# A four-row matmul operand padded to 128 rows, tap weights turned by matmul, and a new written-out order in a one-core SSM and MLP kernel

## The chip, the cores and the metric

The kernel runs on one core of one Trainium2 chip. A core has five engines that run their own instruction streams side by side: TensorE (PE: matmuls and the weight loads for them), VectorE (DVE), ScalarE (ACT), GpSimd (POOL) and SyncE (SP, which here only issues DMAs). They share a scratch memory of 128 rows (partitions), and TensorE writes its results to eight accumulator banks (PSUM). Engines wait for each other and for DMAs on semaphores. The metric is the device time of one execution in microseconds, median of several runs.

## The reference

Two branches over the same input x = A_q (2048 positions, 640 channels, bf16) are mixed by a sigmoid gate:

```python
def _A_ref(q, k, v, shift_k, ssm_k, ssm_D):
    k_pad = jnp.pad(k, ((0, 0), (ks - 1, 0), (0, 0)))
    for t in range(ks):                                   # ks = 4
        k_shift = k_shift + k_pad[:, t:t + S, :] * shift_k[:, ks - 1 - t][None, None, :]
    kv = k_shift * v
    y = irfft2(rfft2(pad(kv)) * rfft2(pad(ssm_k)))[..., :S, :]   # causal convolution per channel
    y = y + kv * ssm_D[None, None, :]
    return q * y

def _B_ref(x, w1, w2, w3, w4):
    h = _gelu(_layernorm(x, axis=-1) @ w1)                # 640 x 640
    # the four quarters of h are shifted by 1, -1, 2, -2 positions
    hs = jnp.concatenate([g0, g1, g2, g3], axis=-1) @ w2  # 640 x 640
    x1 = x + hs
    h2 = _gelu(_layernorm(x1, axis=-1) @ w3) @ w4         # 640 x 1536 x 640
    return x1 + h2

g = _sigmoid((x * gate_w).sum(-1, keepdims=True))
return g * a + (1 - g) * b
```

## The kernel before, in words

All 2048 positions are held in the core's memory as 16 row tiles of 128 (X). The work falls into groups that bear the name of the function that issues them.

Branch B. `x_load` (L843) brings X in; `ln1` (L853) normalises a tile with VectorE's statistics instructions and turns it to channels-first, the first eight tiles by TensorE transposes (L866), the others by SyncE transposing DMAs. `mm1` (L873) is the first product. It has five column blocks: blocks 0 to 3 are the first 128 columns of each quarter, and the fifth block (`w1x`) collects the last 32 columns of all four quarters, so that its gelu is four instructions of 32 rows with four different shifts. The loop at L1066 cuts mm1 into widths of 128 positions for the first chunk of 512 (the fifth block in 256), 256 for the second, 512 for the last two. `mmg` (L887) makes the gate's dot products; `mm2` (L905) the second product, whose result VectorE adds to X (L919) from tile 4 on; `ln2` (L923) normalises again and turns by DMA; `mm3` (L928) and `mm4` (L949) are the MLP; `base` (L944) writes scaled x1.

Branch A. `h_load`, `h_fold` and `h_chunk` (L745) make the spectrum of the filter, 128 channels at a time in five chunks: the 2048 taps are cut into four blocks of 512, folded into even and odd halves on VectorE, turned by DMA, and multiplied with constant DFT matrices on TensorE. `h_fold` also copies row 0 of the turned result to a small tile `hsp` (L743). `h_chunk` uses it as the moving operand of a correction of four rows, whose stationary operand `Zs` is four rows too:

```python
    Zs = AR[0:4, oUT + 4224:oUT + 4480].rearrange("p (j f) -> p j f", j=2)
    hsp = [AR[0:4, o:o + 512] for o in (oUT + 4480, oUT + 4992)]
...
                    if r == 0:
                        pairs.append((Zs[:, j, :], ex))
```

This comes to two matmuls of four rows by 512 columns in each of five chunks. The DFT constants around `Zs` are loaded by the DMA `Rh` from a table of 1920 columns over all rows, `Zs` among them. `kv_load` and `kv_chunk` (L777) do the same for k and v, with the four taps of the shift as per-channel scalars `wk`; `x_fwd` (L790) is their transform; `combine` and `unit` (L960 on) the products of the spectra on VectorE with accumulating DMAs from GpSimd; `final` (L1021) the inverse transform, 16 groups, which TensorE, ScalarE and VectorE finish and which SyncE or GpSimd write or accumulate to the output.

At the start, VectorE sets constants, among them a tile of ones of 640 columns (L671) in which `warm` matmuls run (WARM = 15, L675), and 26 `fill` matmuls (L679) are strewn among the first real ones; none of them makes a result that is used. The taps `shift_k` (640 x 4) are brought by a DMA to `wkb` in channel order (128 rows, five groups of four elements of two bytes, so runs of 8 bytes) and copied to `wk`. `dcol` (L710) turns `ssm_D` and `gate_w`, each loaded as five rows of 128, into columns by two matmuls with five rows.

What sets the order: the program is first recorded as a list of operations, each with the tiles that it reads and writes. The list SEQUENCE, written out by hand as numbers, then gives the order in which they are issued, over all engines and DMA queues; each engine runs its own share of that list in order. The list PLACES gives each accumulator tile its bank. `schedule` (L255) adds to the first user of a bank a wait for the last reader of the tile that held it, and `emit` (L276) turns all dependences into semaphore waits, leaving out those that are implied. Helpers record most instructions, so that matmuls have the line L647, VectorE's tensor-tensor operations L627, ScalarE's L637 and DMAs L238 or (transposes) L235.

Of the kernel before, what the change touches and what calls it, by code (L numbers as in the profile page):

```python
# [422 lines left out]
def bass_gated_mix__ssm_conv_h3__mixer_s_mlp__prompt_kernel(  # L423
# [23 lines left out]
    def V(o, n):  # L447
        return AR[:, o:o + n]
# [7 lines left out]
    def ps(n, cls):  # L456
# [3 lines left out]
    SEQUENCE = [74, 1, 11, 54, 76, 53, 9, 0, 12, 73, 5, 13, 75, 14, 67, 15, 156, 57, 80, 16, 157, 81, 17, 56, 61, 96,  # L460
# [59 lines left out]

# [645 lines left out]
```

## Time and profile before

| what | value |
|---|---|
| median of 3 runs | 229.17 us (228.46 to 234.25) |
| profiled execution | 229.3 us, its span 227.5 us |
| TensorE busy | 217.7 us, 96% of the span, 1437 matmuls |
| VectorE busy | 205.8 us, 90% |
| ScalarE busy | 175.5 us, 77% |
| GpSimd busy | 96.1 us, 42% |
| TensorE idle for VectorE's tensor-tensor operations | 1.4 us, three times |
| TensorE idle for w1's DMA | 0.7 us, once |

The times of the trace count from the start of the span in microseconds. A row of a group gives line, engine, operation, the tiles written and read, the shape, the count, then busy time and the mean length of one in ns, and the idle time of the engine just ahead of such instructions with what ended it. A row of the timeline gives start, length, engine, line and how many instructions follow each other there. Matmuls overlap: the time from issue to issue is shorter than the length of one. The chain that ended last goes from the last instruction back, at each step to what released it.

### The profile page before, as it was taken

How to read it: one execution, taken by the hardware profiler on the slowest of the kernel's cores; microseconds unless marked ns; L12 is line 12 of the kernel's file. 1: busy time of each engine (PE TensorE's matmuls, PEld its weight loads, DVE VectorE, ACT ScalarE, POOL GpSimd, SP SyncE). 2: the span in 40 equal slices, each digit the busy share in tenths (PEclk: the TensorE clock that was granted, in tenths of full speed). 3: DMA queues.
4: the chain of work that ended last, by engine and by line, in shares of the span. 5: the costliest groups of instructions: out<-in, count | busy, mean ns of one | idle time of the engine just before them, and what ended most of it. 6: DMA issues, size and time to landing. Idle time of an engine off the chain costs nothing.

```text
span 227.5 us, 3881 instructions
## 1 busy us (share of the span) xinstructions
PE 217.7 (96%) x1437; PEld 128.5 (56%) x1437; DVE 205.8 (90%) x339; ACT 175.5 (77%) x315; POOL 96.1 (42%) x111
## 2 busy tenths in 40 slices
PE   6989999999999999999999999999999999999970
PEld 2578776554445644446764466665477644677730
DVE  5989998989988989799999999989899999996691
ACT  2279899799999779999976995838987379745970
POOL 0332333263014340000147648297696344357771
PEclk9999999999999999999999999999999999999995
DMA  5999999999999998999679999799999999989997
GB/s 168 280 233 314 197 260 225 179 223 265 216 178 248 194 294 184 278 218 148 179 158 126 208 238 186 158 168 173 269 191 145 240 181 185 176 113 129 124 135 129
DMA packets 81007, 45.01 MB, mean 198 GB/s; under 512 B 59976, under 2 KB 75868, under 8 KB 80988
## 3 DMA queue, kind: packets, MB, share of 16 engines
q1 hardware_dynamic: 71560, 31.92, 62.4%
q0 software_dynamic: 9264, 12.78, 38.2%
q8 instruction: 11, 0.18, 0.3%
q10 hardware_dynamic: 164, 0.07, 0.1%
q14 instruction: 8, 0.07, 0.1%
HBM read 14.92 MB, written 6.55 MB: 94 GB/s over the span
## 4 chain that ended last, share of the span: by engine, by line
PE 88%; DVE 4%; DMA 3%; SPq 2%; ACT 1%; issue 1%
PE PSall L647 86%; DVE arena L627 4%; DMA arena<-in_B_w_dram 3%; SPq L238 2%; PE PSall L679 1%; ACT arena L637 1%; PE PSall L866 1%
## 5 line engine op out<-in xcount | busy, mean ns | idle before, releaser
L647 PE MATMUL PSall<-arena 128*128 128x320 bf16 (+5 forms) x1354 | 205.8, 310 | 2.1 <-DVE arena L627 1.4
L647 PEld LDWEIGHTS PSall<-arena 128*128 128x128 bf16 (+1 forms) x1354 | 122.1, 98 | 85.8 <-issue 6.4
L627 DVE TENSOR_TENSOR arena<-arena 128x2560 bf16<-128x2560 bf16 (+6 forms) x198 | 160.8, 863 | 8.9 <-ACT arena L637 7.0
L637 ACT ACTIVATE arena<-PSall 128x512 bf16<-128x512 f32 (+7 forms) x182 | 105.4, 626 | 26.1 <-PE PSall L647 18.2
L637 ACT ACTIVATE arena<-arena 128x640 bf16<-128x640 bf16 (+5 forms) x75 | 53.9, 740 | 9.2 <-DVE arena L627 8.2
L815 POOL TENSOR_TENSOR arena<-arena 128x1 f32<-128x1 f32 (+2 forms) x17 | 22.6, 1338 | 45.4 <-DVE arena L826 37.7
L238 POOL DMA_DIRECT2D out_dram<-arena x28 | 32.6, 1446 | 19.9 <-ACT arena L637 10.6
L637 ACT ACTIVATE arena<-PSall,arena 128x640 bf16<-128x640 f32 (+1 forms) x32 | 20.6, 655 | 10.2 <-PE PSall L647 10.0
L238 POOL DMA_DIRECT2D arena<-arena x15 | 19.1, 1332 | 18.8 <-DVE arena L627 14.8
L627 POOL TENSOR_TENSOR arena<-arena 128x4 bf16<-128x4 bf16 (+3 forms) x26 | 15.5, 606 | 22.2 <-DVE arena L627 19.4
L632 DVE TENSOR_SCALAR arena<-arena 128x640 bf16<-128x640 bf16 (+3 forms) x45 | 23.3, 541 | 0.9 <-POOL arena L815 0.6
L632 POOL TENSOR_SCALAR arena<-arena 128x2 f32<-128x2 f32 (+4 forms) x21 | 14.4, 689 | 19.9 <-DVE arena L627 9.5
L811 DVE BATCH_NORM_STATS2 arena<-arena 128x6 f32<-128x320 bf16 x32 | 14.3, 477 | 2.3 <-DMA arena<-in_A_q_dram 2.1
L919 DVE SCALAR_TENSOR_TENSOR arena<-PSall,arena 128x640 bf16<-128x640 f32 x12 | 9.7, 817 | 1.6 <-PE PSall L647 1.6
L675 PE MATMUL PSall<-arena 128*128 128x512 bf16 x15 | 5.8, 574 | 1.7 <-DVE arena L671 1.7
L679 PE MATMUL PSall<-arena 128*128 128x512 bf16 x26 | 7.4, 379 | 0.0
L675 PEld LDWEIGHTS PSall<-arena 128*128 128x128 bf16 x15 | 2.0, 139 | 5.1 <-issue 3.2
L866 PE MATMUL PSall<-arena 128*128 128x128 bf16 x40 | 3.4, 219 | 0.0
L866 PEld LDWEIGHTS PSall<-arena 128*128 128x128 bf16 x40 | 2.7, 98 | 0.5
L679 PEld LDWEIGHTS PSall<-arena 128*128 128x128 bf16 x26 | 2.3, 97 | 1.1
L637 ACT ACTIVATE PSall<-PSall 128x640 f32<-128x640 f32 x4 | 2.8, 708 | 0.0
L812 DVE BATCH_NORM_AGGREGATE arena<-arena 128x2 f32<-128x12 f32 x16 | 2.8, 194 | 0.0
(26 smaller groups left out, 10.5 us busy)
## 6 DMA issues: line engine op xcount, KB each, us to landing
arena<-arena POOLq DMA_DIRECT2D x12, 640.0 KB, 6.4
arena<-in_A_q_dram SPq DMA_DIRECT2D x14, 320.0 KB, 4.8
out_dram<-arena POOLq DMA_DIRECT2D x20, 160.0 KB, 4.5
arena<-in_A_ssm_k_dram SPq DMA_DIRECT2D x5, 512.0 KB, 4.5
arena<-in_B_w_dram SPq DMA_DIRECT2D x4, 480.0 KB, 4.6
out_dram<-arena SPq DMA_DIRECT2D x10, 160.0 KB, 4.2
arena<-in_B_w_dram SPq DMA_DIRECT2D x1, 1152.0 KB, 6.0
out_dram<-arena SPq DMA_DIRECT2D x12, 80.0 KB, 2.4
```

The lines of the kernel that those rows point to most:

```text
L238: fn = lambda e: e.dma_start(out, in_, **kw)
L627: P.op(eng, lambda e: e.tensor_tensor(o, real(a), real(b), op), [a, b], [o], dve_ns(o, [a, b], 2) if eng == "dve" else 500)
L632: P.op(eng, lambda e: e.tensor_scalar(o, real(a), s1, s2, op0=op0, **({} if op1 is None else {"op1": op1})), [a] + aps, [o], dve_ns(o, [a] ...
L637: P.op("act", lambda e: e.activation(real(o), real(a), f, bias=bias, scale=scale, **({"accum_out": accum} if accum is not None else {})), ...
L647: fns.append(lambda e, l=l, r=r, i=i: e.matmul(real(o), l, r, start=(i == 0), stop=(i == last)))
L675: P.op("pe", lambda e: e.matmul(real(pw), warm[:, 0:128], warm[:, 128:640], start=True, stop=True), [warm], [pw], 427.0 if i < 14 else 216.0)
L679: P.op("pe", lambda e: e.matmul(real(pw), warm[:, 0:128], warm[:, 128:640], start=True, stop=True), [warm], [pw], 216.0)
L811: P.op("dve", lambda e, o=o, i=i: e.bn_stats(o, i), [i], [o], 400)
L812: P.op("dve", lambda e: e.bn_aggr(bna[:, t, :], bns[k]), [bns[k]], [bna[:, t, :]], 120)
L815: P.op("pool", lambda g: g.tensor_tensor(o, a, e, ALU.pow), [a, e], [o], dur)
L866: P.op("pe", [lambda e, c=c, pb=pb, xn=xn: e.transpose(real(pb)[:, 128 * c:128 * (c + 1)], xn[:, 128 * c:128 * (c + 1)], ident) for c in r ...
L919: P.op("dve", lambda e: e.scalar_tensor_tensor(x, real(pr), 1.0, x, op0=ALU.mult, op1=ALU.add, accum_out=st[1, 0][:, t:t + 1]), [pr, x], [ ...
```

## The change

- The four-row operands `Zs` and `hsp` become tiles of 128 rows. `hsp` is zeroed once at the start by VectorE; the DMA of `h_fold` still writes its rows 0 to 3. The rows of `Zs` below the fourth come with the table that holds it.
- `shift_k` is loaded as five rows of 512 elements (128 channels with four taps each) beside `ssm_D` and `gate_w`. Four five-row matmuls with a stride of four turn the taps to columns in an accumulator tile, from which `wk` is copied. `wkb` goes.
- The tile of ones has 512 columns, not 640.
- The fifth column block of mm1 is done once for each chunk of 512 positions.
- 20 fillers, not 26.
- SEQUENCE and PLACES are written anew. In the new order the X rows and shift_k stand ahead of w1 in SyncE's queue and two more rows of X between w1's halves; 5 of 20 fillers, before 15 of 26, stand behind the first matmul that needs w1's second half; mm2 of tile 12 is followed directly by a part of h_chunk 3 in the same banks (PLACES 0); nine finals, before eight, have their inverse transform behind the last mm4.

```diff
-    SEQUENCE = [74, 1, 11, 54, 76, 53, 9, 0, 12, 73, 5, 13, 75, 14, 67, 15, 156, 57, 80, 16, 157, 81, 17, 56, 61, 96,
...
+    SEQUENCE = [71, 1, 13, 52, 70, 5, 6, 12, 14, 53, 73, 7, 9, 0, 2, 11, 15, 50, 72, 8, 16, 49, 149, 17, 148, 77, 18,
...
-    Zs = AR[0:4, oUT + 4224:oUT + 4480].rearrange("p (j f) -> p j f", j=2)
-    hsp = [AR[0:4, o:o + 512] for o in (oUT + 4480, oUT + 4992)]
+    Zs = V(oUT + 4224, 256).rearrange("p (j f) -> p j f", j=2)
+    hsp = [V(o, 512) for o in (oUT + 4480, oUT + 4992)]
...
-    dg5 = AR[0:5, oXN + 640:oXN + 896]
+    dg5 = AR[0:5, oXN + 512:oXN + 1280]
...
-    wkb = bfs[:, 0:20].rearrange("p (c j) -> p c j", c=5)
...
+    for h in hsp:
+        P.op("dve", lambda e, h=h: e.memset(h, 0.0), [], [h], 230)
     WARM = 15
-    FILL = 26
+    FILL = 20
     const("warm")
-    P.op("dve", lambda e: e.memset(V(oXN, 640), 1.0), [], [V(oXN, 640)], 230)
-    warm = V(oXN, 640)
+    P.op("dve", lambda e: e.memset(V(oXN, 512), 1.0), [], [V(oXN, 512)], 230)
+    warm = V(oXN, 512)
...
     const("shk")
-    P.dma(sp, wkb, A_shift_k.rearrange("(c p) j -> p c j", p=128), slow=True)
+    P.dma(sp, dg5[:, 256:768], A_shift_k.rearrange("(c p) j -> c (p j)", p=128))
...
     const("taps")
-    ts(wk, wkb, 1.0, None, ALU.mult)
+    pk = ps(1, "set")[:, 0:20].rearrange("p (j c) -> p j c", j=4)
+    P.op("pe", [lambda e, j=j: e.matmul(real(pk)[:, j], dg5[:, 256 + j:768:4], ident[0:5, 0:5], start=True, stop=True) for j in range(4)],
+         [dg5[:, 256:768], ident], [pk], 120)
+    ts(wk, pk.rearrange("p j c -> p c j"), 1.0, None, ALU.mult)
...
-        P.dma(sp, hsp[c % 2].rearrange("p (a n) -> p a n", a=1), het[c % 2][0:1].rearrange("p e b c -> p e (b c)"))
+        P.dma(sp, hsp[c % 2][0:4].rearrange("p (a n) -> p a n", a=1), het[c % 2][0:1].rearrange("p e b c -> p e (b c)"))
...
             for t in range(4):
                 at(mm1, 0, 128 * t, 128, range(4))
-                if t % 2:
-                    at(mm1, 0, 128 * (t - 1), 256, (4,))
+            at(mm1, 0, 0, 512, (4,))
         else:
             n = 256 if sc < 2 else 512
             for t in range(512 * sc, 512 * sc + 512, n):
-                at(mm1, sc, t, n)
+                at(mm1, sc, t, n, range(4))
+            at(mm1, sc, 512 * sc, 512, (4,))
```

More of the change, by code (lines that the diff above doesn't have):

```diff
@@ L458, in ps @@
         return v if n == 1 else v.rearrange("p (b n) -> p b n", b=2)
-    SEQUENCE = [74, 1, 11, 54, 76, 53, 9, 0, 12, 73, 5, 13, 75, 14, 67, 15, 156, 57, 80, 16, 157, 81, 17, 56, 61, 96,
[59 rows of a table removed]
-    PLACES = [0, 1, 6, 3, 2, 1, 7, 4, 7, 3, 3, 5, 6, 5, 4, 5, 6, 7, 1, 1, 1, 1, 1, 2, 2, 5, 6, 6, 3, 5, 4, 4, 0, 7, 2,
[5 rows of a table removed]
+    SEQUENCE = [71, 1, 13, 52, 70, 5, 6, 12, 14, 53, 73, 7, 9, 0, 2, 11, 15, 50, 72, 8, 16, 49, 149, 17, 148, 77, 18,
[58 rows of a table added]
+    PLACES = [0, 5, 1, 4, 2, 3, 4, 5, 2, 6, 1, 7, 6, 5, 7, 5, 6, 4, 6, 7, 2, 1, 0, 3, 5, 1, 3, 7, 5, 3, 7, 2, 4, 4, 4,
[5 rows of a table added]
     HW = S + 4
@@ L667, in bass_gated_mix__ssm_conv_h3__mixer_s_mlp__prompt_kernel @@
         P.op("dve", lambda e, i=i: e.memset(krev[i][:, :, :, 0:1], 0.0), [], [krev[i][:, :, :, 0:1]], 70)
+    for h in hsp:
+        P.op("dve", lambda e, h=h: e.memset(h, 0.0), [], [h], 230)
     WARM = 15
-    FILL = 26
+    FILL = 20
     const("warm")
-    P.op("dve", lambda e: e.memset(V(oXN, 640), 1.0), [], [V(oXN, 640)], 230)
-    warm = V(oXN, 640)
+    P.op("dve", lambda e: e.memset(V(oXN, 512), 1.0), [], [V(oXN, 512)], 230)
+    warm = V(oXN, 512)
     pw = ps(1, "warm")
     for i in range(WARM):
-        P.op("pe", lambda e: e.matmul(real(pw), warm[:, 0:128], warm[:, 128:640], start=True, stop=True),
+        P.op("pe", lambda e: e.matmul(real(pw), warm[:, 0:128], warm[:, 0:512], start=True, stop=True),
              [warm], [pw], 427.0 if i < 14 else 216.0)
@@ L678, in bass_gated_mix__ssm_conv_h3__mixer_s_mlp__prompt_kernel @@
         const("fill%d" % i)
-        P.op("pe", lambda e: e.matmul(real(pw), warm[:, 0:128], warm[:, 128:640], start=True, stop=True), [warm], [pw], 216.0)
+        P.op("pe", lambda e: e.matmul(real(pw), warm[:, 0:128], warm[:, 0:512], start=True, stop=True), [warm], [pw], 216.0)
     const("gelu")
@@ L710, in bass_gated_mix__ssm_conv_h3__mixer_s_mlp__prompt_kernel @@
     P.op("pe", [lambda e, i=i: e.matmul(real(pr)[:, 5 * i:5 * i + 5], dg5[:, 128 * i:128 * (i + 1)], ident[0:5, 0:5], start=True, stop=True) for i in range(2)],
-         [dg5, ident], [pr], 60)
+         [dg5[:, 0:256], ident], [pr], 60)
     act(dgT, pr, ACTF.Copy)
```

127 rows, old and new, of tables (PLACES, SEQUENCE) are left out of this document.

## The prediction

> **What bounds the kernel now.** I read the head of the page first, then the chain that ended last in order of time, then the waits of TensorE.
>
> ```profile
> span 227.5 us, 3881 instructions
> PE 217.7 (96%) x1437; PEld 128.5 (56%) x1437; DVE 205.8 (90%) x339; ACT 175.5 (77%) x315; POOL 96.1 (42%) x111
> GB/s 168 280 233 314 197 260 225 179 223 265 216 178 248 194 294 184 278 218 148 179 158 126 208 238 186 158 168 173 269 191 145 240 181 185 176 113 129 124 135 129
> PEclk9999999999999999999999999999999999999995
> ```
>
> TensorE is busy for 96% of the span at an undisturbed clock. VectorE at 90% is the nearest other bound; ScalarE and the queues are farther off. The chain, in order of time, says where the busy engine is also the one that sets the end:
>
> ```profile
> 4.58 7.51 DMA arena<-in_B_w_dram
> 12.09 0.14 issue
> 12.23 0.44 PE PSall L647 x5
> ...
> 29.23 182.58 PE PSall L647 x1133
> ...
> 222.73 0.49 DVE arena L627
> ```
>
> From 12.23, when the second half of w1 has landed, the chain is TensorE alone to 211.8 us, one piece of it 182.58 us and 1133 matmuls long with no other engine between. Behind that a tail of ScalarE, VectorE and the last write ends the span. So an instruction's worth of TensorE time that is saved anywhere from 12 to 212 us comes off the end whole, unless the next operand is late then. The waits of TensorE:
>
> ```profile
> PE PSall L675 <- DVE arena L671: 1.7, 1, 1.7
> PE PSall L647 <- DVE arena L627: 1.4, 3, 0.9
> PE PSall L647 <- DMA arena<-in_B_w_dram: 0.7, 1, 0.7
> ```
>
> The 1.7 is the start (the ones for the warming matmuls), the 1.4 stands in the tail, and the 0.7 is the w1 wait at 12.23. That is all: the present order is without stalls, so any wait that the new order adds shows in full.
>
> **The change part by part.** All sums are made against the profiled execution, 229.3 us (span 227.5 and 1.8 outside it), which stands 0.1 from the median 229.17.
>
> *Padding the four-row operand.* First what a full matmul takes from issue to issue, then a stretch with one matmul of four rows in it:
>
> ```profile
> 87.73 2.54 PE L647 MATMUL PSall<-arena 128*128 128x512 bf16 x11
> 79.93 1.45 PE L647 MATMUL PSall<-arena 128*128 128x512 bf16 x5
> L647 PE MATMUL PSall<-arena 128*128 128x512 bf16 x4 | 1.2, 382 | 0.0
> L647 PE MATMUL PSall<-arena 4*128 4x512 bf16 x1 | 0.4, 385 | 0.0
> L647 PE MATMUL PSall<-arena 4*128 4x512 bf16 x10 | 3.8, 385 | 0.0
> ```
>
> Eleven in 2.54 us, the last 0.38 of it one matmul's own length: (2.54 - 0.38) / 10 = 0.216 each. The second stretch is five, and the two rows under it (the same window by shape) show that one of them has four rows: 1.45 - 0.385 - 4 x 0.216 = 0.20 us more than five full ones take. The durations are alike, 382 and 385 ns, so the loss lies between the instructions, on entering and on leaving the small shape. With all 128 rows nothing changes shape: 10 x 0.20 = **-2.0 us**, all ten standing before 90 us where TensorE is saturated. [...]
>
> Its price is two memsets of 128x512 on VectorE at the very start:
>
> ```profile
> 1.07 0.59 DVE L671 MEMSET arena<- 128x640 bf16 x1
> 3.43 2.86 DVE L811 BATCH_NORM_STATS2 arena<-arena 128x6 f32<-128x320 bf16 x6 [1.71 <-DMA arena<-in_A_q_dram]
> ```
>
> At most 2 x 0.59, at least half that; VectorE idles 1.71 us ahead of 3.43 for its first input, which hides either. I take 0; if they stood ahead of the ones instead, TensorE would start up to 1.2 us late. The ones themselves shrink from 640 to 512 columns, 0.12 of 0.59 us: **-0.1 us** at the start.
>
> *Taps turned by matmul.* Two five-row matmuls stand between fillers already:
>
> ```profile
> 7.62 0.59 PE L679 MATMUL PSall<-arena 128*128 128x512 bf16 x2
> 8.15 0.20 PE L710 MATMUL PSall<-arena 5*128 5x5 bf16 x2
> 8.28 0.60 PE L679 MATMUL PSall<-arena 128*128 128x512 bf16 x2
> ```
>
> From 7.62 to 8.28 is 0.66 us; two fillers take 0.43 of it, so the pair costs 0.23. A second one inside the pair adds about 0.04, so four cost **+0.3 us**, on the path because they now stand among the first product's matmuls, behind w1.
>
> *Fillers.* 26 become 20:
>
> ```profile
> 9.13 1.46 PE L679 MATMUL PSall<-arena 128*128 128x512 bf16 x6
> 10.84 0.72 PE L866 MATMUL PSall<-arena 128*128 128x128 bf16 x10
> ```
>
> (1.46 - 0.38) / 5 = 0.216 again. Six fewer are **-1.3 us**, if TensorE has work to put there. In the old order 15 fillers stand behind the w1 wait, in the new one 5, so ten go from the saturated part and four are added before the wait, which the next item counts.
>
> *The w1 wait.* The last ten matmuls before it issue from 10.84 on at 0.056 each (0.72 less the last one's own 0.22, over 9), so TensorE has nothing from 11.40 to 12.23: 0.83 us lost before. In the new order it has 5 more fillers and 5 more transposes and 5 fewer one-column matmuls (0.025 each) ahead of the first matmul on the second half: 11.40 + 1.08 + 0.28 - 0.12 - 0.12 (earlier start) = 12.5 us. SyncE's queue:
>
> ```profile
> 4.07 1.04 SPq L238 DMA_DIRECT2D arena<-in_B_w_dram  x2
> 5.15 0.92 SPq L238 DMA_DIRECT2D arena<-in_A_shift_k_dram  x1
> 6.11 2.95 SPq L238 DMA_DIRECT2D arena<-in_B_w_dram  x1
> ```
>
> The old order sends both halves at 4.07 and 4.58. The new one puts two more rows of X (320 KB) between them and takes one 40 KB piece of w2 away; 280 KB at the 280 GB/s of the second slice is 1.0 us, so the half lands at 12.09 + 1.0 = 13.1. The wait becomes 0.6: **-0.2 us** net. That shift_k no longer costs the queue its 0.92 and then most of the 2.95 helps what is queued behind it, nothing on the path by itself.
>
> *Fifth block in 512s.* The columns are the same, and so is TensorE's time. ScalarE's four-row gelus go from the first form to the second:
>
> ```profile
> L637 ACT ACTIVATE arena<-PSall 32x256 bf16<-32x256 f32 x16 | 5.9, 374 | 0.4 <-PE PSall L647 0.3
> L637 ACT ACTIVATE arena<-PSall 32x512 bf16<-32x512 f32 x8 | 4.7, 588 | 0.3 <-PE PSall L647 0.2
> ```
>
> 5.9 us in sixteen become 4.7 in eight, -1.2 on an engine 77% busy: hidden, 0.
>
> *The new order.* Three waits come with it. (a) In the new list the second half of mm2 (L905) of row tile 12 is followed at once by a matmul of h_chunk 3 (L745) in the same PSUM bank pair, which must wait until VectorE has added that tile:
>
> ```profile
> L919 DVE SCALAR_TENSOR_TENSOR arena<-PSall,arena 128x640 bf16<-128x640 f32 x12 | 9.7, 817 | 1.6 <-PE PSall L647 1.6
> ```
>
> 0.82 and some 0.2 until the signals have passed, with no matmul in between: **+1.0 us** at about 80 us. The old order has no such pair. (b) SyncE's transposes:
>
> ```profile
> 24.58 4.44 SPq L235 DMA_TRANSPOSE arena<-arena  x2
> 52.00 6.21 SPq L235 DMA_TRANSPOSE arena<-arena  x3
> DMA to landing us min/median/max: 3.6/3.6/3.6
> ```
>
> From 24.58 on this queue is full until 60 us; the last transpose for the first product's chunk 3 leaves the queue at about 58.2 and lands 3.6 after its issue (third row). In the new list the same items stand ahead of it less one, and by the sum of their issue times it is issued at about 56.05 and lands at 59.7. TensorE, 3 us ahead by the savings above, wants it at 59.0 to 59.2: **+0.5 us**. (c) VectorE is given more of its work early, which is a rival below; I cost it at 0 beyond these.
>
> *The tail.* In the new list nine finals stand behind the last mm4, not eight, which lengthens TensorE's end by what it shortens ahead of it, and VectorE's by about 0.2. The last transfer is smaller:
>
> ```profile
> out_dram<-arena SPq DMA_DIRECT2D x10, 160.0 KB, 4.2
> out_dram<-arena SPq DMA_DIRECT2D x12, 80.0 KB, 2.4
> ```
>
> Before, one of the first kind is the last. Now one of the second kind is, and one of the first is issued 0.5 us sooner, which ends last: -0.5 of 1.8 at most. Net **-0.2 us** (between +0.2 and -0.5).
>
> Sum: -2.0 - 0.1 + 0.3 - 1.3 - 0.2 + 1.0 + 0.5 - 0.2 = -2.0, so **227.3 us**.
>
> **The rivals.**
>
> *VectorE holds the banks (228.6).* By the sum of the durations that stand ahead of them, the evacuations of mm2 tiles 4 to 6 come 0.0 to 0.4 us after TensorE wants their banks, at 37 to 49 us, even if VectorE never idles; in the old order they are 1 us before it.
>
> ```profile
> 3.43:49.30 45.87, 45.18 (x389) 29.71 (x388) 43.13 (x114) 34.65 (x82) 15.90 (x27) 1.00 1.10 242
> ```
>
> The columns after the length are PE, PEld, DVE, ACT and POOL: VectorE is busy 43.13 of 45.87 us, so it idled 2.7. Half of that kept makes TensorE wait 1.4 + 0.4 = 1.8, of which the 0.5 of (b) is then not paid again: +1.3. Against it: with more put early, there are fewer gaps to idle in.
>
> *The padding gives nothing (229.3).* If the 0.20 belongs to the accumulating pair or to the place and not to the four rows, -2.0 falls away. Against it: the five-row pair shows a like cost in another place.
>
> *SyncE's queue becomes the bound (230.5, slower).* Its run of transposes must not slip. The load of V shows what one slip costs:
>
> ```profile
> 19.16 5.38 SPq L235 DMA_TRANSPOSE arena<-in_A_v_dram  x1
> 58.25 2.18 SPq L235 DMA_TRANSPOSE arena<-in_A_k_dram  x1
> ```
>
> Two transposes of one size, 5.38 and 2.18 us. One more of the long kind ahead of 56 us puts the landing at 62.9, and TensorE waits one for one: +3.2. The break-even is 2.0 us of slip; two such slips would pass 2% above. For it: the new list puts loads of the next k, v and filter rows among the fold transposes. Against it: shift_k's 3 us of blocking is gone ahead of them.
>
> *The new waits do not appear (225.2).* If w1's half lands as early as it does now, the queue keeps its slack, and the mm2 bank is read sooner, 0.6 + 0.5 + 1.0 fall away. For it: every one is a sum over engines that could run earlier. Against it: (a) has no cover at all.
>
> **How the numbers follow.** Forecast 227.3 (226.3 to 228.2): 0.54. VectorE holds the banks: 0.17. Padding worth nothing: 0.05. Queue bound: 0.12. No new waits: 0.12. Eight in ten: from the 225.0 of the favourable case to 230.0, which leaves out the worse half of the queue's case and the lower part of the favourable one. Two per cent (224.6 and 233.75) is about what a measurement of this kernel can tell from no change. Faster by over 2% needs the favourable case and another 0.6 (0.07); slower by over 2% needs two slips in the queue or several cases at once (0.05).
>
> **What the profile of the changed kernel would show.** Padding: no four-row form, and stretches of 512 columns with 0.216 throughout. Fillers and w1: TensorE waits about 0.6 for w1 at 12.5, not 0.8 at 11.4. (a): one TensorE wait for L919's line of about 1.0 near 80 us. (b): a wait of 0.5 for a transpose near 59. (c): waits for VectorE between 37 and 50 in its place, if the rival holds. Tail: VectorE's last row ends at 221 to 222, not at 223.2, and the last write has 80 KB. I would be wrong if TensorE's chain from 12.5 on is broken in other places, for example at h_fold 0's transposes near 33.5, which by the sums arrive 0.3 us before they are wanted.

## The result and the profile after

The changed kernel takes 240.47 us (239.93 to 240.66), the kernel before 228.87 beside it: 1.051 times as long (95% interval 1.048 to 1.054). It is slower by 11.6 us where 2 us less was forecast. The head of its page, with the share of the chain that ended last:

```profile
span 238.1 us, 3854 instructions
PE 217.8 (91%) x1425; PEld 126.8 (53%) x1425; DVE 206.9 (87%) x341; ACT 172.9 (73%) x307; POOL 93.0 (39%) x111
PE   7999999999999899999989159999999999999970
ACT  2299978878997999998385089368984556834981
PEclk9999999999999999999999859999999999999997
PE 58%; ACT 9%; DVE 8%; DMA 6%; POOL 2%; issue 1%; ACTq 0%
```

TensorE's busy time is as before (217.8 us, 217.7 before), but its share of the span fell from 96 to 91%, and there is one hole in its row, in slices 22 and 23 of 40 (131 to 143 us), where the granted clock falls too, to 0.8 and 0.5. The chain, which was 88% TensorE, is now 58%. So the time did not go into instructions but into one wait. TensorE's waits:

```profile
PE PSall L645 <- ACT arena L635: 9.0, 3, 7.8
PE PSall L675 <- DVE arena L671: 1.6, 1, 1.6
PE PSall L645 <- DVE arena L625: 1.5, 2, 0.8
PE PSall L645 <- DVE arena L922: 0.9, 1, 0.9
PE PSall L645 <- ACT PSall L635: 0.5, 1, 0.5
```

The 0.9 for L922 is the bank of mm2 tile 12, forecast at 1.0. The first row is new: 7.8 us in one piece, for ScalarE. What ScalarE did meanwhile, from its timeline (start, length, and in brackets its idle time ahead and what ended it):

```profile
111.96 1.06 ACT L635 ACTIVATE arena<-arena 128x1024 bf16<-128x1024 bf16 x1 [0.57 <-DVE arena L625]
116.82 2.45 ACT L635 ACTIVATE arena<-arena 128x640 bf16<-128x640 bf16 x3 [3.80 <-POOL arena L625]
...
128.98 0.74 ACT L635 ACTIVATE arena<-arena 128x640 bf16<-128x640 bf16 x1 [1.89 <-DMA arena<-arena]
...
129.71 0.58 ACT L635 ACTIVATE arena<-PSall 128x512 bf16<-128x512 f32 x1
136.96 0.74 ACT L635 ACTIVATE arena<-arena 128x640 bf16<-128x640 bf16 x1 [6.67 <-DMA arena<-arena]
...
137.69 3.50 ACT L635 ACTIVATE arena<-PSall 128x512 bf16<-128x512 f32 x7
```

It stood still too. The instructions at 128.98 and 136.96 are the squares of mm2 tiles 12 and 13 (their sums feed ln2); their elementwise result is not used, but it is written to the two buffers `xn2` that the transposes of ln2 tiles 10 and 11 still read. Behind them in ScalarE's queue stand seven gelus of mm3 1 (the last row) that were ready: they would have emptied the banks that TensorE waited for. Why the transposes were late begins 20 us earlier, at 116.82, where ScalarE waited 3.80 us for GpSimd before it could scale ln2 tiles 8 and 9. GpSimd's timeline, of the kernel after and then of the kernel before:

```profile
110.87 5.30 POOL L818 TENSOR_TENSOR arena<-arena 128x4 f32<-128x4 f32 x1 [24.82 <-DVE arena L829]
116.25 0.54 POOL L625 TENSOR_TENSOR arena<-arena 128x4 f32<-128x4 f32 x1
```

```profile
113.05 1.47 POOL L815 TENSOR_TENSOR arena<-arena 128x4 f32<-128x4 f32 x1 [30.64 <-DVE arena L826]
```

The same instruction, the power of four numbers per row in ln_math 8 to 12 (the one over square root of the layernorm), took 1.47 us before and 5.30 after. That the hole costs more than its length shows in the second half of it and in the stretch behind it (columns as in the prediction's window row, then clock, share and rate of the DMAs):

```profile
132.00:135.70 3.70, 0.00 (x0) 0.00 (x0) 0.00 (x0) 0.00 (x0) 0.00 (x0) 1.00 1.13 71
135.74:139.79 4.05, 0.00 (x1) 0.01 (x1) 1.97 (x3) 2.83 (x7) 1.73 (x2) 0.50 0.61 114
139.80:142.50 2.70, 2.70 (x7) 1.03 (x8) 2.67 (x3) 1.75 (x4) 2.58 (x3) 0.50 0.00 0
```

TensorE's last matmul ahead of the hole ends at 132.0, the granted clock is 1.00 until 135.7, 3.7 us later, and 0.50 from there. TensorE comes back at half its clock for 2.7 us; half of that, some 1.3 us, is lost by estimate. Of the runs below only the one with another long wait (6.4 us, the sum one place earlier) has a clock like that: 0.50 from 139.8 to 142.5, and 0.980 in the mean of the profiled execution, against 0.978 here. In the other ten no wait of TensorE is over 1.7 us, and the mean is 0.987 to 0.995 (0.987 in the kernel before).

### The profile page after: what moved, and what is told of

Read it like the earlier page. It is cut to its first block, busy times and chain, and to the rows that moved or that the text cites. A ratio compares the mean times of both kernels' runs of the same rounds, so it can differ in the third digit from the quotient of the medians.

```text
span 238.1 us, 3854 instructions
## 1 busy us (share of the span) xinstructions
PE 217.8 (91%) x1425; PEld 126.8 (53%) x1425; DVE 206.9 (87%) x341; ACT 172.9 (73%) x307; POOL 93.0 (39%) x111
## 4 chain that ended last, share of the span: by engine, by line
PE 58%; ACT 9%; DVE 8%; DMA 6%; POOL 2%; issue 1%; ACTq 0%
PE PSall L645 58%; ACT arena L635 9%; DVE arena L625 7%; DMA arena<-arena 6%; POOL arena L818 2%; DVE arena L630 1%; DVE arena L922 0%; ACT PSall L635 0%; POOL arena L625 0%; DVE arena L829 0%; ACTq L364 0%
## 5 line engine op out<-in xcount | busy, mean ns | idle before, releaser
L645 PE MATMUL PSall<-arena 128*128 128x320 bf16 (+4 forms) x1344 | 206.1, 312 | 12.3 <-ACT arena L635 9.0
L645 PEld LDWEIGHTS PSall<-arena 128*128 128x128 bf16 x1344 | 120.7, 98 | 96.6 <-ACT arena L635 16.1
L635 ACT ACTIVATE arena<-arena 128x640 bf16<-128x640 bf16 (+5 forms) x75 | 54.9, 758 | 16.1 <-DMA arena<-arena 9.3
L818 POOL TENSOR_TENSOR arena<-arena 128x1 f32<-128x1 f32 (+2 forms) x17 | 20.2, 1206 | 49.2 <-DVE arena L829 40.7
L238 POOL DMA_DIRECT2D out_dram<-arena x28 | 30.2, 1197 | 19.4 <-ACT arena L635 16.0
L238 POOL DMA_DIRECT2D arena<-arena x15 | 17.5, 1169 | 30.8 <-DVE arena L625 24.3
L630 DVE TENSOR_SCALAR arena<-arena 128x640 bf16<-128x640 bf16 (+2 forms) x44 | 23.5, 551 | 1.7 <-POOL arena L818 0.9
L630 POOL TENSOR_SCALAR arena<-arena 128x2 f32<-128x2 f32 (+4 forms) x21 | 13.2, 631 | 17.2 <-DVE arena L922 7.7
L922 DVE SCALAR_TENSOR_TENSOR arena<-PSall,arena 128x640 bf16<-128x640 f32 x12 | 9.7, 817 | 1.8 <-PE PSall L645 1.8
L829 DVE SCALAR_TENSOR_TENSOR arena<-arena 128x1 f32<-128x1 f32 (+1 forms) x7 | 1.1, 155 | 11.7 <-ACT arena L635 11.7
L675 PE MATMUL PSall<-arena 128*128 128x512 bf16 x15 | 5.6, 554 | 1.6 <-DVE arena L671 1.6
L679 PE MATMUL PSall<-arena 128*128 128x512 bf16 x20 | 5.5, 380 | 0.0
L675 PEld LDWEIGHTS PSall<-arena 128*128 128x128 bf16 x15 | 1.9, 136 | 4.7 <-issue 2.9
L869 PEld LDWEIGHTS PSall<-arena 128*128 128x128 bf16 x40 | 2.7, 98 | 1.8 <-DVE arena L630 1.2
(29 smaller groups left out, 12.6 us busy)
```

Source lines behind the costliest of these rows:

```text
L238: fn = lambda e: e.dma_start(out, in_, **kw)
L630: P.op(eng, lambda e: e.tensor_scalar(o, real(a), s1, s2, op0=op0, **({} if op1 is None else {"op1": op1})), [a] + aps, [o], dve_ns(o, [a] ...
L635: P.op("act", lambda e: e.activation(real(o), real(a), f, bias=bias, scale=scale, **({"accum_out": accum} if accum is not None else {})), ...
L645: fns.append(lambda e, l=l, r=r, i=i: e.matmul(real(o), l, r, start=(i == 0), stop=(i == last)))
L675: P.op("pe", lambda e: e.matmul(real(pw), warm[:, 0:128], warm[:, 0:512], start=True, stop=True), [warm], [pw], 427.0 if i < 14 else 216.0)
L679: P.op("pe", lambda e: e.matmul(real(pw), warm[:, 0:128], warm[:, 0:512], start=True, stop=True), [warm], [pw], 216.0)
```

## The experiments

The theory has two links: GpSimd's slow power makes the ln2 chain late (1), and the squares, ahead of ready gelus in ScalarE's queue, turn that into a TensorE stall (2). The rivals were that the transposes are late for another reason, or that the power is slow by itself. Apart from that, the prediction's own steps were tried one by one. All ratios are to the kernel before, run beside.

### The squares write elsewhere

```diff
-        act(xn2[t % 2], X[:, t, :], ACTF.Square, scale=D ** -0.5, accum=st[1, 1][:, t:t + 1])
+        act(xn2[t % 2] if t < 12 else V(oXT + 2560 + 640 * (t % 4), 640), X[:, t, :], ACTF.Square, scale=D ** -0.5, accum=st[1, 1][:, t:t + 1])
```

> The changed kernel, but the squares of mm2 tiles 12 to 15 (ScalarE) write their unused result where that tile's transposed result will lie later, not into the two buffers that the transposes of ln2 tiles 10 and 11 still read. Theory A (ScalarE stands in its queue at the squares of tiles 12 and 13, waiting for those transposes, with the gelus of mm3 1 behind it, and TensorE runs out of banks): the wait of 7.8 us before 139.8 goes and with it the slow clock behind it (3 us at half speed, 1.3 us): 240.4 - 9.1 = 231.3. Rival B (the transposes themselves are late and are what everything needs): TensorE stands instead where mm3 2 wants the same transposes, and the time stays above 236.

Measured: 232.39 us, 1.014 (1.010 to 1.019). The waits of TensorE:

```profile
PE PSall L645 <- DVE arena L625: 2.9, 3, 1.4
PE PSall L645 <- ACT arena L635: 2.5, 5, 1.0
```

The 7.8 is gone; apart from the start nothing over 1.4 is left, and the time falls by 8.1 of 11.6 us. Link (2) holds. It is a point of what ScalarE's queue waits for, not of the transposes, which this run did not make earlier: by the trace's semaphore records that of ln2 tile 11 lands at 136.9 in both. The new 1.4 stands at 194.8, for VectorE: some of the lateness was only passed on.

### VectorE waits for the power

```diff
-        tt(kv, kv, vT, ALU.mult)
+        if c == 4:
+            P.op("dve", lambda e: e.tensor_tensor(kv, kv, vT, ALU.mult), [kv, vT, st[1, 5][:, 8:12]], [kv], 1132)
+        else:
+            tt(kv, kv, vT, ALU.mult)
```

and in SEQUENCE the power stands directly behind its sum, ahead of this product.

> The changed kernel, but the last product of kv_chunk 4 on VectorE, which follows the sum of ln_math 8 to 12, also waits for GpSimd's power of that sum. Theory C (GpSimd's power took 5.3 us because VectorE ran without a gap beside it, and this is the first delay of the chain): the power takes 1.5 us or less, VectorE loses as much, ln2 tiles 8 to 11 come 4 us earlier and the 7.8 us wait becomes 3.8 or less: 236 or below. Rival D (the power is slow for a reason of its own): it still takes about 5 us, VectorE waits 5 us, and the time is 240 or more.

Measured: 229.83 us, 1.003 (1.000 to 1.006). GpSimd's power and VectorE's product behind it:

```profile
110.96 1.04 POOL L822 TENSOR_TENSOR arena<-arena 128x4 f32<-128x4 f32 x1 [24.83 <-DVE arena L833]
112.03 1.23 DVE L790 TENSOR_TENSOR arena<-arena 128x2048 bf16<-128x2048 bf16 x1 [1.15 <-POOL arena L822]
```

With VectorE standing still the power takes 1.04 us, not 5.30, and a *wait added* to an engine that was busy without a gap makes the kernel 10.6 us faster. Link (1) holds, and the power is not slow by itself.

### The sum one place earlier, and a gap by order alone

What lets GpSimd in? In the trace of after, VectorE's instructions overlap by 0.08 us from 110.7 on; the first that does not is the one at 115.30, which waits for the result of the one directly before it:

```profile
114.59 0.68 DVE L625 TENSOR_TENSOR arena<-arena 128x1024 bf16<-128x1024 bf16 x1
115.30 0.69 DVE L625 TENSOR_TENSOR arena<-arena 128x1024 bf16<-128x1024 bf16 x1
```

114.59 + 0.68 = 115.27: a gap of 0.03. The power ended 0.87 behind it, at 116.17. Two orders of VectorE test that, with no wait added:

```diff
 # the first: the sum (494) ahead of a product of unit 0 3
-..., 699, 764, 763, 494, 700, ...
+..., 699, 764, 494, 763, 700, ...
 # the second: the fourth tap's sum (699) directly ahead of the product that needs it (700)
-..., 699, 764, 763, 494, 700, ...
+..., 764, 763, 494, 699, 700, ...
```

(VectorE's operations alone are shown, by their numbers in SEQUENCE.)

> The changed kernel with the small sum of ln_math 8 to 12 one instruction earlier on VectorE, ahead of a product of 2560 columns; no wait added. Theory C1 (GpSimd's power gets through only where VectorE leaves a gap, and the first gap stands ahead of the instruction that waits for the one directly before it, near 115.3): the power starts at about 109.3, lasts 6.5 to 7 us and ends where it ended before, near 116.2; the time stays at 240. Theory C2 (it is delayed by so much work or takes so long, 5.3 us): it ends at 114.6, the chain behind it comes 1.5 us earlier, and the time falls by 1.5 or more.

> The changed kernel with one sum of kv_chunk 4 moved on VectorE from two places ahead of the small sum of ln_math 8 to 12 to directly behind it, so that it stands directly ahead of the product that needs it; no wait is added that was not there. Theory C1 (any gap that VectorE leaves for its own predecessor lets GpSimd in): the power takes about 2.1 us (1.2 to the gap, 0.9 behind it) in place of 5.3, and the 7.8 us wait of TensorE goes: about 230. Rival (the wait for the power itself was what helped in the run before): the power stays above 4 us and the time at 238 to 240.

Measured: 239.36 us, 1.044 (1.038 to 1.050) for the first. Its power:

```profile
110.54 6.70 POOL L819 TENSOR_TENSOR arena<-arena 128x4 f32<-128x4 f32 x1 [23.44 <-DVE arena L830]
```

It lasts longer by as much as VectorE's extra product (1.40) and again ends 0.87 us behind the start of the first instruction after a gap (116.38 here, the end at 117.24). The second takes 228.25 us, 0.998 (0.995 to 1.000), with

```profile
109.16 1.96 POOL L819 TENSOR_TENSOR arena<-arena 128x4 f32<-128x4 f32 x1 [23.82 <-DVE arena L830]
```

that is 1.09 us until the gap and 0.87 behind it, about as worked out (1.2 and 0.9). The instruction behind the gap is a 128x1024 sum in the two slow cases and a 128x2048 product here, so it is the gap and not that instruction's shape. One instruction moved behind three others on an engine takes 12.2 us off, and apart from the start TensorE has no wait of over a microsecond left.

The power came 3.8 us late, and the hole was 7.8 us long. What lies between shows in the DMAs, those of the changed kernel first and then those of the second order:

```profile
124.27 1.54 POOL L238 DMA_DIRECT2D arena<-arena  x1
126.28 1.19 POOL L238 DMA_DIRECT2D arena<-arena  x1 [0.48 <-DVE arena L625]
126.41 1.99 SPq L235 DMA_TRANSPOSE arena<-arena  x1
```

```profile
122.00 1.20 SPq L235 DMA_TRANSPOSE arena<-arena  x1
122.93 1.22 POOL L238 DMA_DIRECT2D arena<-arena  x1 [1.77 <-DVE arena L626]
```

The transpose is that of ln2 tile 11; the others are GpSimd's accumulating DMAs of 640 KB. By the semaphore records the transpose lands 10.5 us after its issue in the changed kernel, at 136.9, and 2.9 us after it in the second order, at 124.9: 4.4 us of lateness at the issue became 12 at the landing. In the new order it took 9.1 to 11.3 us in the three kernels in which the first of these DMAs goes ahead of it (the changed one and those with the squares elsewhere and the sum earlier), and 2.7 to 4.3 in the other five, where it goes ahead of both. That these DMAs slow it fits that, but no run tests it alone, and in the old order the last of the four transposes took 4.0 to 8.4 us ahead of both.

### The padding alone, in the old order

```diff
-    Zs = AR[0:4, oUT + 4224:oUT + 4480].rearrange("p (j f) -> p j f", j=2)
-    hsp = [AR[0:4, o:o + 512] for o in (oUT + 4480, oUT + 4992)]
+    Zs = V(oUT + 4224, 256).rearrange("p (j f) -> p j f", j=2)
+    hsp = [V(o, 512) for o in (oUT + 4480, oUT + 4992)]
...
+    for h in hsp:
+        P.op("dve", lambda e, h=h: e.memset(h, 0.0), [], [h], 230)
...
```

> The kernel before with the padded operands and their two memsets alone, in the old order. If ten four-row matmuls cost 0.20 us each beside full ones, TensorE's stream is 2.0 us shorter and no other wait is near: 228.9 - 2.0 = 226.9. If the row count makes no difference: 228.9. If the old order has no slack for an earlier TensorE: 227.5 to 228.5.

Measured: 227.97 us, 0.995 (0.993 to 0.997), 1.2 us less. None of the ten places where the interval between starts was 0.10 us too long going in and 0.10 coming out is left in the trace, so the 2.0 is saved on TensorE. But there is a wait that the kernel before did not have:

```profile
PE PSall L648 <- DVE arena L922: 0.7, 1, 0.7
```

It stands at 50.7, for the evacuation of mm2 tile 7 (VectorE adds the tile to X and so empties its bank). 2.0 - 0.7 = 1.3, against 1.2 measured.

### The padding undone in the new order

The second of the two orders above, with four-row operands again (the diff of the section before, the other way round, but the two memsets stay, on four rows).

> The changed kernel with the one sum moved on VectorE, and the operands four rows high again (memsets on four rows). If ten matmuls at 0.20 us each cost in this order what they cost in the old one: 228.3 + 2.0 = 230.3. If the waits that the earlier TensorE meets in this order (some 1.8 us of them between 33 and 78) are shorter when it comes later: 229 to 229.7.

Measured: 229.65 us, 1.002 (0.999 to 1.005), against 228.25 and 0.998 with the padding: 1.0 by the ratios and 1.4 by the medians, so half to two thirds of the 2.0 arrives in this order.

### The parts in the old order

Padding, 512-wide ones, the taps by matmul and 20 fillers, in the old SEQUENCE; the fifth block as before. The new operations stand here:

```diff
-..., fill 10, mm1 0 128 (w1's first half), transposes of ln1, mm1 0 128 (w1's second half), ...
+..., fill 10, taps (four matmuls), mm1 0 128 (w1's first half), transposes of ln1, mm1 0 128 (w1's second half), ...
```

> The kernel before in its old order with the padding, the 512-wide ones, the taps turned by four five-row matmuls ahead of the w1 wait, and 20 fillers (the last six of 26 left out); the fifth block stays as it was. If the parts do what the sum of the prediction gives them and the loss is all in the new order: -2.0 - 1.3 and nothing for the taps, which the wait for w1 hides: 228.9 - 3.3 = 225.6. If an earlier TensorE meets late operands in the old order too: 227 to 229, with new waits of TensorE that add up to the difference.

Measured: 228.12 us, 0.994 (0.991 to 0.996). A wait took part of it:

```profile
PE PSall L711 <- DMA arena<-in_A_shift_k_dram: 1.3, 1, 1.3
```

In the old queue shift_k is issued behind w1, and the wait for it ends at 10.87; the taps stood too early for it. The next run moves them behind the transposes, in the place where TensorE waits for w1 anyway:

> The run with the parts in the old order, with the taps' four matmuls moved from 1.3 us ahead of shift_k's landing to just ahead of the matmul that waits for w1's second half. Theory (TensorE's stream sets the end, and only the waits on it matter): the 1.3 us wait goes and the wait for w1 comes back with less than 0.8, the taps inside it: 228.1 - 0.6 to 1.3, that is 226.8 to 227.5. Rival (VectorE sets the end in the old order as well, once TensorE is 3 us shorter): 228.1 as before, with a longer wait for VectorE near 50 us.

Measured: 227.62 us, 0.993 (0.990 to 0.997). Of TensorE's timeline:

```profile
11.71 0.29 PE L711 MATMUL PSall<-arena 5*128 5x5 bf16 x4 [0.54 <-DMA arena<-in_A_shift_k_dram]
50.68 167.56 PE L648 MATMUL PSall<-arena 128*128 128x512 bf16 x1026 [0.77 <-DVE arena L925]
```

The first wait is down to 0.54, and none for w1 is left, but the one for mm2 tile 7 has grown from 0.2 to 0.77: 0.6 of the 0.8 gained is given back 40 us later. That evacuation stands on VectorE behind a layernorm scaling that waits 0.62 us for GpSimd. So it was put ahead of it:

```diff
-..., kv_chunk 1, ln1 14 16 (scaling), mm2 7 (evacuation), ...
+..., kv_chunk 1, mm2 7 (evacuation), ln1 14 16 (scaling), ...
```

> The run with the parts in the old order and the taps later, with VectorE's evacuation of mm2 tile 7 one instruction earlier, ahead of a layernorm scaling that waits 0.6 us for GpSimd. Theory (the new wait of 0.77 near 50 us is this evacuation standing behind a stalled instruction): the wait goes, 227.6 - 0.7 = 226.9. Rival (VectorE's total work sets the end): 227.6, with the time given back later.

Measured: 227.41 us, 0.991 (0.988 to 0.995). The wait at 50.68 is gone, and there is another at

```profile
53.22 165.62 PE L648 MATMUL PSall<-arena 128*128 128x512 bf16 x1006 [0.67 <-DVE arena L633]
```

The step to 227.62 lies inside the intervals. This run has the lowest median of all, 0.9% below the kernel before and 5.7% below the changed one, with the old order and most of the change's parts.

### More waits taken out of the new order

Two edits on the run in which VectorE waits: the squares' own place, and h_chunk 4's first matmuls ahead of those of h_chunk 3 that wait for mm2 tile 12's bank (416 and 417 ahead of 386 on TensorE, 418 ahead of 388 on ScalarE).

> The run in which VectorE waits for GpSimd's power, with two more edits: the squares of tiles 12 to 15 write to their own place, and h_chunk 4's first matmuls stand ahead of those of h_chunk 3 that wait for the bank of mm2 tile 12. If TensorE sets the end: the waits of 1.0 before 130.9 and of 0.9 before 78.6 (0.2 left) go, 229.8 - 1.7 = 228.1. If VectorE, whose order is unchanged, sets the end by now: 229 to 230, with the waits turning up at later places.

Measured: 229.68 us, 1.002 (1.000 to 1.005), no gain at all over 229.83:

```profile
78.88 1.47 PE L646 MATMUL PSall<-arena 128*128 128x512 bf16 x6 [0.56 <-ACT arena L636]
81.16 109.54 PE L646 MATMUL PSall<-arena 128*128 128x320 bf16 x635 [0.81 <-ACT arena L636]
191.72 27.62 PE L646 MATMUL PSall<-arena 128*128 128x320 bf16 x195 [1.02 <-DVE arena L626]
```

The 0.93 near 78 became 0.56 + 0.81 for ScalarE, the 1.0 near 131 turned up as 1.02 for VectorE at 191.7. A second try, on the run with the gap by order, gave the three tiles other banks instead:

```diff
 # PLACES: bank pair of the tiles; in SEQUENCE the second matmul of the h_chunk 3 tile (387)
 # also goes ahead of the first one of the h_chunk 4 tile (416)
-h_chunk 3 (the tile behind mm2 12): 0    h_chunk 4 (the next): 4    mm2 15: 0
+h_chunk 3 (the tile behind mm2 12): 4    h_chunk 4 (the next): 0    mm2 15: 4
```

> The changed kernel with the one sum moved on VectorE (the run in which the gap comes by order alone), and three accumulator tiles in other banks: the h_chunk 3 tile that had to wait for mm2 tile 12 goes to the pair that is free, that of h_chunk 4 behind it takes the pair of mm2 12, mm2 tile 15 follows h_chunk 3. Theory (the bank is what TensorE waits 0.93 us for near 78, and nothing else is late there): the wait falls to 0.3 or less, 228.3 - 0.6 = 227.6. Rival (the wait moves on to ScalarE's or VectorE's next evacuation, as in the run with two edits at this place): 228.3, with new waits between 79 and 87.

Measured: 228.22 us, 0.995 (0.992 to 0.997), against 228.25 and 0.998: nothing by the medians, 0.7 us by the ratios, whose intervals overlap. The 0.93 fell to 0.28, with 0.35 behind it for ScalarE:

```profile
78.14 1.04 PE L647 MATMUL PSall<-arena 128*128 128x512 bf16 x4 [0.28 <-DVE arena L924]
79.52 110.87 PE L647 MATMUL PSall<-arena 128*128 128x512 bf16 x645 [0.35 <-ACT arena L637]
190.80 27.62 PE L647 MATMUL PSall<-arena 128*128 128x320 bf16 x195 [0.41 <-DVE arena L627]
```

In both tries most of what TensorE gained was asked back by the engines that empty its banks.

## Why the prediction was wrong

The step that failed is the sentence "Three waits come with it" under the new order. The list was incomplete, and every term in it was made from durations of the kernel before, as if an instruction's length went with it to another place. The power of ln_math 8 to 12 took 1.47 us there and 5.30 in the new order, and the transpose behind it 10.5 us to land; together they made a wait of 7.8 us at 132, of which the list has nothing. None of the rivals had it; only the sign of being wrong that the prediction names for itself, a TensorE chain broken in other places, is what came. The slower one (230.5, SyncE's transposes slipping ahead of 56 us) was not it: the transposes that were late are ln2's, 70 us behind those, and VectorE's order alone brings the time back. A second point was missed in the same step: I looked for what TensorE waits for directly, and not for ScalarE instructions whose only wait is a buffer that a DMA still reads. In the old order the squares of tiles 12 and 13 stood behind at least seven of mm3 1's twelve gelus, in the new one ahead of at least eight.

Point by point:

- **Padding, -2.0.** Right on TensorE, in both orders: no interval of the old kind is left. On the end it is worth 1.2 in the old order and 1.0 to 1.4 in the new one: in the old order a new wait of 0.7 for VectorE takes the rest. "The padding gives nothing" is out.
- **Fillers, taps and start.** With the padding they gave 1.1 to 1.6 us in the old order where 3.3 was set; part of the difference stands in named waits (1.3 for shift_k, then 0.5 and 0.8, less the 0.7 for w1 that is gone), and the rest is not accounted for.
- **The w1 wait, 0.6.** TensorE's list of waits in the changed kernel has no row for w1; in the run with the gap by order it is 0.31. Over-sized: w1's half landed at 12.0 and 12.6 in these two, not at 13.1. (In the new list 4 of the 20 fillers, not 5, stand behind it, so five more stand ahead of it, as the sum of 12.5 has it, and not four.)
- **(a) mm2 tile 12's bank, 1.0.** 0.93: 0.82 for VectorE's evacuation, and 0.04 ahead of it and 0.07 behind it for the signals, where some 0.2 was set. Right; but taking it away yields between nothing and 0.7.
- **(b) SyncE's transposes, 0.5.** No row of that kind. Over-sized.
- **(c) VectorE early, 0.** Between 37 and 50 no row of TensorE's waits names it. What was missed at 34 is 0.5 for ScalarE, which squares mm2's result in the bank that h_chunk 0 wants.
- **The tail, -0.2.** From VectorE's last instruction to the end of the span it is 4.3 us before, 4.0 in the changed kernel and 4.1 in the run with the gap by order. About right.
- **The sum.** With the one VectorE sum moved, the changed kernel takes 228.25, 0.95 over the forecast of 227.3, just above the 226.3 to 228.2 set for this case. It is 0.5 us (by the ratio) to 0.8 (by the medians) faster than the kernel before where 2.0 was forecast. So the rest of the sum has the right sign and delivers less than half of its size, with terms that erred both ways; the 12.2 us are one event that it had no term for.

## What to carry to other kernels

An order that is moved can change the lengths of instructions, not only their starts: GpSimd's power took 1.47 us in one order, 5.30 in another and 1.96 with one sum moved. So look at the short instructions on the critical chain that stand beside an engine that runs without a gap, and give them a gap, by order if possible; here that was worth 12.2 us. An instruction whose result is not used should not be written where a DMA still reads, least of all ahead of ready work in its engine's queue: two squares that were held up so cost 8.1 us. And a microsecond saved on TensorE, busy for 96% of the span, was worth about half of it at the end here, because waits for a load and for the engines that empty its banks took the rest.

## What the runs showed of the hardware that was not expected

GpSimd's small tensor-tensor instruction was held off by VectorE for as long as VectorE issued without a gap: it took 5.30, 6.70 and 1.96 us in three orders, and 1.04 with VectorE idle. The kernel before has a case of its own, harmless there. GpSimd, then VectorE:

```profile
154.83 6.33 POOL L815 TENSOR_TENSOR arena<-arena 128x1 f32<-128x1 f32 x1 [1.68 <-DVE arena L826]
```

```profile
154.66 6.06 DVE L627 TENSOR_TENSOR arena<-arena 128x2560 bf16<-128x2560 bf16 x7
161.71 0.49 DVE L627 TENSOR_TENSOR arena<-arena 128x640 bf16<-128x640 bf16 x1 [0.98 <-ACT arena L637]
```

It ends at 161.16, 0.44 behind the end of VectorE's run of seven (160.72). In the slow cases here GpSimd did not get in at the ends of VectorE's instructions, four of which lie between 110.87 and 115.0 in the changed kernel, but only at a gap of 0.03 us or more. An instruction that waits for the one directly before it made such a gap (115.27 to 115.30), and here a wait for ScalarE did (0.98 us). Why GpSimd has to wait there was not shown. What stays open: some powers got through in 1.4 to 1.8 us beside VectorE with no such gap in its rows (the 1.47 at 113.05 and the 1.75 at 130.12 are two). The shape of VectorE's instructions alone does not decide it: two 128x1024 instructions back to back let GpSimd in there (112.93 and 113.54), and two others of that size in the changed kernel did not (113.99 and 114.59). What does was not tried.
